# Unfolded odd units in the first batch, whole loads in the last

## Chip, cores and metric

The kernel runs on one core of a Trainium2 chip. The metric is the device time of one execution in microseconds (us), as the median of several runs.

## What is computed

Eight sequences of 3136 rows by 256 go through a Fourier layer and then a routed feed-forward layer. Of the reference this matters here (shortened):

```python
X = np.fft.rfft(x, axis=1)                      # 3136 rows
Yr = Xr @ w_r - Xi @ w_i + b_r
Yi = Xr @ w_i + Xi @ w_r + b_i
Yr, Yi = softshrink(Yr, 0.01), softshrink(Yi, 0.01)
y = np.fft.irfft(Yr + 1j * Yi, n=3136, axis=1)
scores = np.einsum('bsd,d->bs', y, w_gate)
for b in range(8):                              # top 128 rows of each batch
    xe = y[b, top_idx]
    ye = np.maximum(xe @ w1, 0.0) @ w2
    out[b, top_idx] = xe + sigmoid(scores[b, top_idx])[:, None] * ye
```

## The kernel before

The transform of 3136 = 98 x 32 points is done in two steps each way, all as small float32 matmuls.

**Stage one** (`s1`, 8 units per batch, two units to one load of 784 KB). `ld_x` brings 98 rows of 8 KB into a tile, `xt` or `cv`. `fold` forms the sum and the difference of the two halves of x (`sd`, two buffers, two instructions per unit, on VectorE or GpSimd). `s1` multiplies them by the table `w` (four matmuls in the source, eight records in the trace), ScalarE copies the result to `at` (or `ot`), and after each second unit SyncE stores 784 KB to `As` in HBM. PSUM tile `s` takes the even units of batch 0 and `px` the odd ones.

**Stage two** runs over 100 steps: `s2` (second transform step, from `As` through `ld_a` into `av`), `spectral` and `shrink` (the complex product with the weights, and the soft threshold), `s2i` (first inverse step, copied to `ct`, stored to `Cs`). **Stage three** (`s1i`, 8 units per batch) loads `Cs` into `cv` and writes the output through `ot`. Behind it `route` selects the 128 rows of a batch (`select`, eight rounds of one digit each, then `place`), `fetch` gathers them into `xe`, `ffn` computes them, and an indirect DMA scatters them.

The order on every engine is the order in which the program text runs (`manual_schedule`). Stores are collected in `stores` and issued by `flush`. SyncE (SP) issues nearly all transfers, in order, and a transfer that waits holds up all behind it. The semaphores of transfers are eight lanes (DMAHW0 to 7), so a transfer may also wait for the one eight before it.

**The start.** SP loads x of batch 0 (four transfers), constants, then stores `As` in four parts; between them stand loads of x for batch 1. `warm(n)` issues n matmuls on a constant to keep TensorE at work. `ld_a(0, 0)` needs all four stores.

**The end.** In the last batch (7), `ld_last(k, late)` loads quarter k of `Cs`. The rows of the last steps (those with a = 4, 5 in groups of six) aren't known when the other rows are, so a quarter came as four transfers of 16 rows with a = 0..3, one of 2 rows, and, after the last two steps' results were stored, two more of 16 rows (`late`). Then the eight `s1i` units of batch 7 run between the rounds of `select` for batch 7 and the feed-forward of batch 6.

Line numbers in the rows: L426 is `s1`, L460 `s2`, L531 the copy in `s2i`, L600 `s1i`, L619 `warm`, L415 `fold`, L254 the matmul of a round of `select`, L245 to L273 its steps on VectorE, L328 the last matmuls of `place`, L378 and L394 the two products of `ffn`, L160 every transfer issued through `ld`, L433 the store of `As`.

Of the kernel before, what the change touches and what calls it, by code (L numbers as in the profile page):

```python
# [27 lines left out]
def _tables():  # L28
    m = np.arange(NH)
    n2 = np.arange(N2)  # L30
    n4 = np.arange(64)
    o4 = 2 * (n4 % 32) + n4 // 32
    wf = np.zeros((64, 2, 64))
    wi = np.zeros((64, 64))
    g = np.zeros((2, 2, N2, NP, 2, 3, N2))
    gi = np.zeros((2, 2, N2, NP, 2, 2, 64))
    for j in range(NJ - 1):
        e = 2 * j + 2
        for p, r in enumerate((e, NH - e if e < NH else 0)):
            a = 2 * np.pi * ((m * r) % N1) / N1  # L40
            wf[:NH, p, 2 * j + 15 - 15 * p] = np.cos(a)
            wf[:NH, p, 2 * j + 16 - 15 * p] = -np.sin(a)
            for k2 in range(N2):
                k = r + 98 * k2
                sg = 1.0 if 2 * k <= S else -1.0
                a = 2 * np.pi * ((n2 * k) % S) / S
                g[j % 2, 0, :, j // 2, p, 0, k2] = np.cos(a)
                g[j % 2, 1, :, j // 2, p, 0, k2] = np.sin(a)
                g[j % 2, 0, :, j // 2, p, 1, k2] = -sg * np.sin(a)
                g[j % 2, 1, :, j // 2, p, 1, k2] = sg * np.cos(a)  # L50
                kk, si = (k, sg) if p == 0 else (S - k, -sg)
# [12 lines left out]
    gt = np.zeros((2, N2, 3, NF))  # L64
    gti = np.zeros((NF, 2, 64))
    slots = [(0, 98 * k2) for k2 in range(17)] + [(1, 49 + 98 * k2) for k2 in range(16)]
    for s, (q, k) in enumerate(slots):
        a = 2 * np.pi * ((n2 * k) % S) / S
        edge = k in (0, S // 2)
        gt[q, :, 0, s] = np.cos(a)  # L70
        gt[q, :, 1, s] = -np.sin(a)
        a = 2 * np.pi * ((n4 * k) % S) / S
        gti[s, 0, o4] = (1.0 if edge else 2.0) * np.cos(a) / S
        gti[s, 1, o4] = (0.0 if edge else -2.0) * np.sin(a) / S
    gt[:, :, 2] = gt[:, :, 0] + gt[:, :, 1]
    wq = np.zeros((2, 2, 32, NH, 2))
    for a in range(2):
        wq[:, a, :24, :, a] = wi[:48, :NH].reshape(24, 2, NH).transpose(1, 0, 2)
        wq[0, a, 24, :, a] = wi[48, :NH]
    near = np.array([2 * (8 * t + j) + a for j in range(8) for t in range(3) for a in range(2)])  # L80
    wc = np.zeros((64, 79))
    wc[:, 15:] = wi
    ws = wc[np.concatenate([near, [NH - 1] + 15 * [63]])]
    wis = np.stack([np.concatenate([np.roll(wc, 15, 0), wc]), np.concatenate([np.roll(wc[np.concatenate([[NH - 1], near, 15 * [63]])], 15, 0), ws])], 1)
    return (np.concatenate([np.roll(wf, 15, 0), wf]), wis, g.reshape(128, NJ - 1, 3 * N2), gi.reshape(128, NP, 2, 128),
            np.concatenate([gt.reshape(NF, 3, NF)] * 2), np.concatenate([gti] * 2), wq.reshape(128, N1))

# [23 lines left out]
def fourier_moe(ctx: ExitStack, tc: tile.TileContext, x, w_r, w_i, b_r, b_i, wg, w1, w2,  # L111
# [17 lines left out]
    def c_tile(shape, dt, name):  # L129
        return const.tile(shape, dt, name=name)  # L130

    w = c_tile([128, 2, NF], F32, "w")
    nc.scalar.dma_start(out=w, in_=t_w)
    wi_sb = c_tile([128, 2, 79], F32, "wi_sb")
    nc.scalar.dma_start(out=wi_sb, in_=t_wi)
    xts, cvs = [[c_tile([128, 8, D], F32, n + str(k)) for k in range(2)] for n in ("xt", "cv")]
    for k, t in enumerate(xts + cvs):
        (nc.vector if k % 2 else nc.gpsimd).memset(t[:15], 0.0)
    g_sb = c_tile([128, NJ - 1, 3 * N2], F32, "g_sb")
    gt_sb = c_tile([128, 3, NF], F32, "gt_sb")  # L140
    wts = [[c_tile([128, 2, D], F32R, n + c) for c in "hl"] for n in ("ws", "wd", "wn")]
# [272 lines left out]
        for k, op in enumerate((ALU.add, ALU.subtract)):  # L414
            eng.tensor_tensor(out=f[:113, k], in0=t[:113, 0], in1=t[:113, 1], op=op)  # L415

    def s1(b, i):
        if i == 0:
            As[b] = dram.tile([2, NH, N2, D], F32, name="As")
        if i % 2 == 0:  # L420
            at[b] = pool.tile([128, 2, 2, 2 * D], F32, name="ot" if b == 0 and i > 3 else "at", bufs=2)
        f = sd.pop((b, i))
        p = ps.tile([128, 2, 2 * D], F32, name="px" if b == 0 and i % 2 else "s", bufs=1)
        for r in range(2):
            for c in range(2):
                nc.tensor.matmul(p[64 * c:64 * c + 64, r, :], w[64 * r:64 + NH * r, c, :], f[64 * r:64 + NH * r, c], start=True, stop=True)  # L426
        t = at[b]
        nc.scalar.copy(out=t[:, :, i % 2, :], in_=p)  # L428
        if i % 2 == 0:
            return  # L430

        def store():
            nc.sync.dma_start(out=As[b].rearrange("q m n d -> (q m) n d")[:, 4 * i - 4:4 * i + 4, :], in_=t[15:113])  # L433
        stores.append(store)
# [68 lines left out]
    def s2i(b, g):  # L503
# [37 lines left out]
        elif b == B - 1 and g in (3, 7, 10, 11):  # L541
            def store():
                lo, n = {10: (0, 6), 11: (6, 8)}.get(g, (0, 8))
                for q in range(2):
                    ld(Cs[b][1 + 48 * q:49 + 48 * q].rearrange("(j t a) n d -> t (a n) j d", t=3, a=2)[g // 4, :, lo:n], t[q::2, lo:n])
            stores.append(store)
        elif b < B - 1 and g % 4 == 3:
            def store():
# [32 lines left out]
            cv[b, i // 2] = cvs[i // 2 % 2]  # L581
            ld(cv[b, i // 2][15:113], Cs[b].rearrange("r m n d -> (r m) n d")[:, 4 * i:4 * i + 8, :])

    def ld_last(k, late):
        t = cv[B - 1, k] = (xts if k < 2 else cvs)[k % 2]
        v = Cs[B - 1][:, 8 * k:8 * k + 8, :]
        for a in (4, 5) if late else range(4):
            ld(t[16 + a:112:6], v[1:N1 - 1].rearrange("(i a) n d -> a i n d", a=6)[a])
        if not late:
            ld(t[15:113:N1 - 1], v[::N1 - 1])  # L590

    def s1i(b, i):
        e = i % 2
# [134 lines left out]

    for i in range(U):
        ld_x(0, i)  # L730
    warm(16)
    consts_a()
    consts_g(0)
    consts_c()
    for i in range(U):
        fold(0, i, nc.gpsimd if i % 3 == 2 else nc.vector)
        s1(0, i)
        flush()
        if i == 5:
            ld_x(1, 0)  # L740
    ld_x(1, 2)
    weights()
    warm(20)
    ld_a(0, 0)
    ld_x(1, 4)
    ld_x(1, 6)
    first = {i - 1: i for i in range(U)}
# [3 lines left out]
    for t in range(-1, T):  # L751
# [6 lines left out]
        for b, i in loads[t] if t >= 0 else ():  # L758
            ld_c(b, i)
        if t > T - 3:  # L760
            for k in (0, 1) if t == T - 2 else (2,):
                ld_last(k, False)
        if t in (0, 4, 8):
            consts_g(t // 4 + 1)
        if t in (-1, 1, 4, 9):
# [62 lines left out]

    while threads or ffns:
        done["t"] = t  # L830
        if t == T:
            ld_last(3, False)
        flush()
        load[0] = 0.0
        if t == T:
# [4 lines left out]
            flush()  # L840
            load[0] = 0.0
            work(0.8, True)
            for k in range(4):
                ld_last(k, True)
        load[0] = 0.0
        turn("pe", "da", "db")
        us = 0.4 if t == T else 1.2 if t < T + 11 else 0.6
# [33 lines left out]
```

## Time and profile before

| | |
|---|---|
| median of 3 runs | 698.41 us |
| lowest, highest | 694.76, 701.81 us |
| profiled execution | 699.96 us |
| its span | 698.2 us |
| mean granted TensorE clock | 0.969 |
| TensorE (PE) busy | 654.1 us, 94% |
| VectorE (DVE), ScalarE (ACT), GpSimd (POOL) busy | 439.2, 364.7, 293.3 us |

The span is what the profiler saw; the 1.76 us by which the execution is longer lie around it. The granted clock is a share of 2.4 GHz: 1.00 is 2.4 GHz and 0.50 is 1.2 GHz.

### The profile page before, as it was taken

How to read it: one execution, taken by the hardware profiler on the slowest of the kernel's cores; microseconds unless marked ns; L12 is line 12 of the kernel's file. 1: busy time of each engine (PE TensorE's matmuls, PEld its weight loads, DVE VectorE, ACT ScalarE, POOL GpSimd, SP SyncE). 2: the span in 40 equal slices, each digit the busy share in tenths (PEclk: the TensorE clock that was granted, in tenths of full speed). 3: DMA queues.
4: the chain of work that ended last, by engine and by line, in shares of the span. 5: the costliest groups of instructions: out<-in, count | busy, mean ns of one | idle time of the engine just before them, and what ended most of it. 6: DMA issues, size and time to landing. Idle time of an engine off the chain costs nothing.

```text
span 698.2 us, 20329 instructions
## 1 busy us (share of the span) xinstructions
PE 654.1 (94%) x8363; PEld 483.3 (69%) x8363; DVE 439.2 (63%) x1388; ACT 364.7 (52%) x672; POOL 293.3 (42%) x247
## 2 busy tenths in 40 slices
PE   5679999999999999999999999999999999998896
PEld 3357766777777777777777777677777777676365
DVE  5526555677687667766667664776577667775330
ACT  2336565566665566654654664556555555553220
POOL 4168555555545555345435544554542222220001
PEclk9799999999999999999999999999999999999569
DMA  8799857798989898988587767879676745776430
GB/s 248 273 242 331 274 165 210 221 309 263 300 251 313 265 299 254 339 234 283 169 262 231 261 215 249 285 240 289 217 224 184 220 140 183 230 230 194 141 120 24
DMA packets 72014, 163.79 MB, mean 235 GB/s; under 512 B 4878, under 2 KB 57584, under 8 KB 59376
## 3 DMA queue, kind: packets, MB, share of 16 engines
q1 hardware_dynamic: 70736, 160.17, 72.8%
q0 software_dynamic: 896, 2.17, 1.0%
q8 instruction: 66, 1.08, 0.6%
q14 instruction: 28, 0.23, 0.1%
q10 hardware_dynamic: 288, 0.15, 0.1%
HBM read 84.42 MB, written 78.12 MB: 233 GB/s over the span
## 4 chain that ended last, share of the span: by engine, by line
PE 63%; DVE 14%; DMA 7%; issue 5%; ACT 5%; POOL 2%; SPq 1%; POOLq 0%; DVEq 0%; ACTq 0%
PE pca L521 10%; PE s L600 6%; DVE junk L533 5%; PE py L233 5%; PE px L460 5%; PE py L234 5%; PE s L426 5%; PE py L235 5%; PE pcb L233 4%; PE m L378 3%; PE m L394 2%; PE pcb L235 2%; PE pcb L234 2%; ACT ct L531 2%; DVE Xl L473 2%
## 5 line engine op out<-in xcount | busy, mean ns | idle before, releaser
L489 POOL TENSOR_TENSOR kb<-ks,bias 128x512 f32<-128x512 f32 x100 | 128.1, 1281 | 308.9 <-ACT ks L487 307.5
L415 POOL TENSOR_TENSOR sd<-xt 113x512 f32<-113x512 f32 x106 | 133.4, 1281 | 23.9 <-DMA xt<-in_x 12.4
L493 DVE TENSOR_TENSOR py<-py,kb 128x512 f32<-128x512 f32 x100 | 70.0, 700 | 77.9 <-POOL kb L489 73.2
L531 ACT COPY ct<-pcb 128x256 f32<-128x256 f32 (+1 forms) x100 | 37.2, 372 | 151.4 <-PE pcb L521 137.1
L521 PE MATMUL pca<-Y,gi_sb 64*64 64x256 f32 x760 | 101.8, 386 | 5.4 <-DVE pca L251 4.8
L473 DVE TENSOR_TENSOR Xl<-px,Xh 128x768 fp32r<-128x768 f32 x100 | 95.8, 958 | 16.7 <-ACT Xh L472 16.5
L521 PE MATMUL pcb<-Y,gi_sb 64*64 64x256 f32 x768 | 103.0, 386 | 0.0
L533 DVE CUSTOM_DVE_ANT_0 junk<-pcb,wgb 128x256 f32<-128x256 f32 (+1 forms) x100 | 42.4, 424 | 87.7 <-ACT ct L531 86.8
L460 PEld LDWEIGHTS px<-g_sb,av 64*64 64x64 f32 x3072 | 78.2, 134 | 17.4 <-issue 3.5
L472 ACT CAST Xh<-px 128x768 fp32r<-128x768 f32 x100 | 81.1, 811 | 13.3 <-PE px L460 11.8
L460 PE MATMUL px<-g_sb,av 64*64 64x96 f32 x3072 | 83.4, 244 | 3.5 <-issue 3.1
L602 ACT COPY ot<-s 128x1024 f32<-128x1024 f32 x58 | 60.1, 1036 | 43.3 <-PE s L600 43.3
L521 PEld LDWEIGHTS pca<-Y,gi_sb 64*64 64x64 f32 x760 | 46.5, 132 | 41.0 <-DVE pca L251 11.7
L498 ACT ACTIVATE r<-py,m2l 128x512 f32<-128x512 f32 x100 | 70.5, 705 | 4.6 <-DVE py L493 4.6
L500 DVE SCALAR_TENSOR_TENSOR Y<-py,r 128x512 f32<-128x512 f32 x100 | 68.5, 685 | 1.6 <-ACT r L498 1.6
L426 PE MATMUL s<-sd,w 64*64 64x512 f32 x480 | 67.4, 607 | 2.2 <-POOL sd L415 1.2
L428 ACT COPY at<-s 128x1024 f32<-128x1024 f32 x58 | 60.6, 1045 | 12.0 <-PE s L426 11.8
L233 PE MATMUL pcb<-wsh,Xh 128*128 128x256 f32 x200 | 65.3, 326 | 1.5 <-DVE Csc L533 1.5
L600 PE MATMUL s<-cv,wi_sb 64*64 64x512 f32 x464 | 63.3, 614 | 0.0
L233 PE MATMUL py<-wnh,Xh 128*128 128x256 f32 x200 | 56.7, 284 | 1.8 <-DVE Y L500 1.7
L234 PE MATMUL pcb<-wsh,Xl 128*128 128x256 f32 x200 | 56.0, 280 | 0.0
L235 PE MATMUL pcb<-wsl,Xh 128*128 128x256 f32 x200 | 55.9, 279 | 0.0
(184 smaller groups left out, 1368.4 us busy)
## 6 DMA issues: line engine op xcount, KB each, us to landing
av<-As SPq DMA_DIRECT2D x46, 512.0 KB
Cs<-ct SPq DMA_DIRECT2D x46, 512.0 KB
As<-at SPq DMA_DIRECT2D x30, 784.0 KB
out<-ot SPq DMA_DIRECT2D x30, 784.0 KB
xt<-in_x SPq DMA_DIRECT2D x28, 784.0 KB
cv<-Cs SPq DMA_DIRECT2D x28, 784.0 KB
cv<-in_x SPq DMA_DIRECT2D x4, 784.0 KB
As<-ot SPq DMA_DIRECT2D x2, 784.0 KB
```

Source lines behind the costliest of these rows:

```text
L233: nc.tensor.matmul(out, wh, mh, start=start, stop=False)
L234: nc.tensor.matmul(out, wl, mh, start=False, stop=False)
L235: return nc.tensor.matmul(out, wh, ml, start=False, stop=stop).ins
L415: eng.tensor_tensor(out=f[:113, k], in0=t[:113, 0], in1=t[:113, 1], op=op)
L426: nc.tensor.matmul(p[64 * c:64 * c + 64, r, :], w[64 * r:64 + NH * r, c, :], f[64 * r:64 + NH * r, c], start=True, stop=True)
L460: nc.tensor.matmul(o[:, :, N2 * j:N2 * j + N2], a[64 * p:64 * p + 64, j, g % 4, 128 * h + 64 * q:128 * h + 64 * q + 64], g_sb[64 * p:64 * ...
L472: nc.scalar.copy(out=vh, in_=v)
L473: nc.vector.tensor_tensor(out=vl, in0=v, in1=vh.bitcast(F32), op=ALU.subtract)
L489: nc.gpsimd.tensor_tensor(out=kb[:r], in0=ks[:r].broadcast_to([r, 2, D]), in1=bias[:r], op=ALU.add)
L521: nc.tensor.matmul(p[q][64 * a:64 * a + 64], gi_sb[64 * q:64 * q + 64, g, c, 64 * a:64 * a + 64], y[64 * q:64 * q + 64, c, :], start=(c == ...
L533: nc.vector.tensor_tensor_reduce(out=junk[:r], in0=p[k][:r], in1=wgb[:r], scale=1.0, scalar=0.0, op0=ALU.mult, op1=ALU.add, accum_out=Csc[ ...
L600: nc.tensor.matmul(p[64 * c:64 * c + 64, r, :], wi_sb[64 * r:64 + NH * r, b // (B - 1), 15 * c:15 * c + 64], f[64 * r:64 + NH * r, 4 * c + ...
```

## The change

Three things change, without the result being another.

In batch 0 the odd units are no longer folded. `w` gets a third column block, the negative of its second, and an odd unit takes the halves of x as they are: the sum as two accumulating matmuls with the same table, the difference as one with the table and one with its negative. An odd unit so has 16 records in place of 8, and is done ahead of the even unit of its pair. The four folds left (two instructions each) are all on VectorE. The four clearing memsets move behind the first `warm`, which is 8 matmuls long in place of 16; the second is 24 in place of 20. `ld_a(0, 0)` moves ahead of the load of x for units 2 and 3 of batch 1.

In batch 7 the first two quarters of `Cs` come in one transfer of 98 rows of 16 KB, the third in one of 98 rows of 8 KB, with all rows, known or not; what is not yet known is then replaced by two transfers of 16 rows of 16 KB and two of 16 rows of 8 KB. The fourth quarter is loaded whole after these. So that the rows hold numbers, the store of step 3 is done twice, to its own rows and to those of the last steps.

```diff
+    wf = np.concatenate([wf, -wf[:, 1:]], 1)
...
-        f = sd.pop((b, i))
...
+        if (b, i) in sd:
+            f = sd.pop((b, i))
+            parts = [[(c, f[:, c])] for c in range(2)]
+        else:
+            f = [xt[b, i // 2][:, h, 2 * e:2 * e + 2, :] for h in range(2)]
+            parts = [[(c, f[0]), (2 * c, f[1])] for c in range(2)]
+        for k in range(len(parts[0])):
+            for r in range(2):
+                for c in range(2):
+                    v, f = parts[c][k]
+                    nc.tensor.matmul(p[64 * c:64 * c + 64, r, :], w[64 * r:64 + NH * r, v, :], f[64 * r:64 + NH * r],
+                                     start=(k == 0), stop=(k == len(parts[0]) - 1))
...
-                for q in range(2):
-                    ld(Cs[b][1 + 48 * q:49 + 48 * q].rearrange("(j t a) n d -> t (a n) j d", t=3, a=2)[g // 4, :, lo:n], t[q::2, lo:n])
+                for k in (0, 2) if g == 3 else (g // 4,):
+                    for q in range(2):
+                        ld(Cs[b][1 + 48 * q:49 + 48 * q].rearrange("(j t a) n d -> t (a n) j d", t=3, a=2)[k, :, lo:n], t[q::2, lo:n])
...
-    def ld_last(k, late):
-        t = cv[B - 1, k] = (xts if k < 2 else cvs)[k % 2]
-        v = Cs[B - 1][:, 8 * k:8 * k + 8, :]
-        for a in (4, 5) if late else range(4):
-            ld(t[16 + a:112:6], v[1:N1 - 1].rearrange("(i a) n d -> a i n d", a=6)[a])
+    def ld_last(k, n, late):
+        t = whole.rearrange("p k n d -> p (k n) d") if k == 0 else cvs[k % 2]
...
+        v = Cs[B - 1][:, 8 * k:8 * k + 8 * n, :]
         if not late:
-            ld(t[15:113:N1 - 1], v[::N1 - 1])
+            ld(t[15:113], v)
+        else:
+            for a in (4, 5):
+                ld(t[16 + a:112:6], v[1:N1 - 1].rearrange("(i a) n d -> a i n d", a=6)[a])
...
-    warm(16)
+    warm(8)
...
-    for i in range(U):
-        fold(0, i, nc.gpsimd if i % 3 == 2 else nc.vector)
-        s1(0, i)
+    for i in range(0, U, 2):
+        fold(0, i, nc.vector)
+        s1(0, i + 1, True)
+        s1(0, i, False)
         flush()
-        if i == 5:
+        if i == 4:
             ld_x(1, 0)
+    weights()
+    warm(24)
+    ld_a(0, 0)
     ld_x(1, 2)
-    weights()
-    warm(20)
-    ld_a(0, 0)
...
-            for k in (0, 1) if t == T - 2 else (2,):
-                ld_last(k, False)
+            ld_last(*((0, 2) if t == T - 2 else (2, 1)), False)
...
-        if t == T:
-            ld_last(3, False)
         flush()
...
-            for k in range(4):
-                ld_last(k, True)
+            ld_last(0, 2, True)
+            ld_last(2, 1, True)
+            ld_last(3, 1, False)
```

Three places show how the instructions move. First TensorE at the start of the program, before, from the first `warm` to the third unit (`px<-Xh` is the warming):

```order
L619 MATMUL px<-Xh 128x512 [waits Activation_49]
L619 MATMUL px<-Xh 128x512 x15
L426 MATMUL s<-sd,w 64x512 [waits DMAHW0_49,DVE_49]
L426 MATMUL s<-sd,w 64x512 [waits DVE_49]
L426 MATMUL s<-sd,w 64x512 x2
L426 MATMUL px<-sd,w 64x512 [waits DVE_49,PE_49]
L426 MATMUL px<-sd,w 64x512 [waits DVE_49]
L426 MATMUL px<-sd,w 64x512 x2
L426 MATMUL s<-sd,w 64x512 [waits Activation_49,Pool_49]
L426 MATMUL s<-sd,w 64x512 [waits Pool_49]
L426 MATMUL s<-sd,w 64x512 x2
```

And the same place now (the odd unit reads `xt` or `cv_83`, which hold x):

```order
L633 MATMUL px<-Xh 128x512 [waits Activation_49]
L633 MATMUL px<-Xh 128x512 x7
L434 MATMUL px<-xt,w 64x512 [waits DMAHW0_49,DMAHW1_49,DVE_49,PE_49]
L434 MATMUL px<-xt,w 64x512 x7
L434 MATMUL s<-sd,w 64x512 [waits DVE_49] x2
L434 MATMUL s<-sd,w 64x512 x2
L434 MATMUL px<-xt,w 64x512 [waits DMAHW3_49,Activation_49,Pool_49]
L434 MATMUL px<-xt,w 64x512 x7
L434 MATMUL s<-sd,w 64x512 [waits DVE_49,Activation_49]
L434 MATMUL s<-sd,w 64x512 [waits DVE_49]
L434 MATMUL s<-sd,w 64x512 x2
```

The odd unit comes first and waits for the load of x and for the table, not for a fold; the warming ahead of it is half as long.

Second, SP at the start, from the first store of `As` to the loads of x for batch 1 (`xt`, `cv` from `in_x`), before:

```order
L433 DMA As<-at 98x2048 [waits DMAHW3_49,Activation_49]
L433 DMA As<-at 98x2048 [waits DMAHW4_49,Activation_49]
L433 DMA As<-ot 98x2048 [waits DMAHW5_49,Activation_49]
L160 DMA xt_82<-in_x 98x2048 [waits DMAHW6_49,DVE_49]
L433 DMA As<-ot 98x2048 [waits DMAHW7_49,Activation_49]
L160 DMA xt_83<-in_x 98x2048 [waits DMAHW0_49,DVE_49,Pool_49]
L160 DMA av<-As 128x2x256 [waits DMAHW5_49,DMAHW4_49,DMAHW7_49,DMAHW3_49,DMAHW1_49]
L160 DMA av<-As 128x2x256 [waits DMAHW2_49]
L160 DMA av<-As 128x2x256 x2
L160 DMA cv_84<-in_x 98x2048 [waits DVE_49,Pool_49]
L160 DMA cv_85<-in_x 98x2048 [waits DMAHW6_49,DVE_49]
```

And now:

```order
L443 DMA As<-at 98x2048 [waits DMAHW3_49,Activation_49]
L443 DMA As<-at 98x2048 [waits DMAHW4_49,Activation_49]
L443 DMA As<-ot 98x2048 [waits DMAHW5_49,Activation_49]
L160 DMA xt<-in_x 98x2048 [waits DMAHW6_49,DVE_49,PE_49]
L443 DMA As<-ot 98x2048 [waits DMAHW7_49,Activation_49]
L160 DMA av<-As 128x2x256 [waits DMAHW5_49,DMAHW4_49,DMAHW7_49,DMAHW3_49,DMAHW0_49]
L160 DMA av<-As 128x2x256 [waits DMAHW1_49]
L160 DMA av<-As 128x2x256 [waits DMAHW2_49]
L160 DMA av<-As 128x2x256
L160 DMA xt<-in_x 98x2048 [waits DVE_49,PE_49]
L160 DMA cv_83<-in_x 98x2048 [waits DVE_49,PE_49]
L160 DMA cv_84<-in_x 98x2048 [waits DMAHW6_49,DVE_49,PE_49]
```

The second load of x into `xt` now stands behind the four loads of `av`.

Third, SP near the end, from the last transfer of the third quarter of `Cs_77` (batch 7) over the fourth quarter to the first late transfer, before (ahead of these stand ten transfers for the first two quarters and four for the third):

```order
L160 DMA cv_84<-Cs_77 2x2048 [waits DMAHW2_49]
L160 DMA cv_85<-Cs_77 16x2048 [waits DMAHW3_49,PE_49]
L160 DMA cv_85<-Cs_77 16x2048 [waits DMAHW4_49]
L160 DMA cv_85<-Cs_77 16x2048 [waits DMAHW5_49]
L160 DMA cv_85<-Cs_77 16x2048 [waits DMAHW6_49]
L160 DMA cv_85<-Cs_77 2x2048 [waits DMAHW7_49]
L160 DMA out<-ot 98x2048 [waits DMAHW0_49,Activation_49]
L160 DMA Cs_77<-ct 64x6x256 [waits DMAHW1_49,Activation_49]
L160 DMA Cs_77<-ct 64x6x256 [waits DMAHW2_49]
L160 DMA Cs_77<-ct 64x2x256 [waits DMAHW3_49,Activation_49]
L160 DMA Cs_77<-ct 64x2x256 [waits DMAHW4_49]
L160 DMA xt_82<-Cs_77 16x2048 [waits DMAHW4_49,DMAHW3_49,DMAHW5_49,DMAHW2_49,DMAHW1_49]
```

And now, with the first three quarters in the first two rows:

```order
L160 DMA xt<-Cs_77 98x4096 [waits DMAHW4_49,DMAHW6_49,DMAHW3_49,Pool_49]
L160 DMA cv_83<-Cs_77 98x2048 [waits DMAHW7_49,DMAHW0_49,PE_49]
L160 DMA out<-ot 98x2048 [waits Activation_49]
L160 DMA Cs_77<-ct 64x6x256 [waits DMAHW6_49,DMAHW7_49,DMAHW1_49,Activation_49]
L160 DMA Cs_77<-ct 64x6x256 [waits DMAHW2_49]
L160 DMA Cs_77<-ct 64x2x256 [waits Activation_49]
L160 DMA Cs_77<-ct 64x2x256
L160 DMA xt<-Cs_77 16x4096 [waits DMAHW4_49,DMAHW3_49,DMAHW5_49,DMAHW2_49,DMAHW1_49]
L160 DMA xt<-Cs_77 16x4096
L160 DMA cv_83<-Cs_77 16x2048
L160 DMA cv_83<-Cs_77 16x2048 [waits DMAHW0_49]
L160 DMA cv_84<-Cs_77 98x2048 [waits PE_49]
```

The first store of the last steps' results, `Cs_77<-ct 64x6x256`, now waits for the lanes of the two whole loads (6 and 7), the output store ahead of it stands behind two transfers in place of twenty, and the fourth quarter comes behind the late transfers.

## Rows read from the trace of the kernel before

**Rows 1.** The page: TensorE in 40 slices, chain by engine.

```profile
PE   5679999999999999999999999999999999998896
...
PE 63%; DVE 14%; DMA 7%; issue 5%; ACT 5%; POOL 2%; SPq 1%; POOLq 0%; DVEq 0%; ACTq 0%
```

**Rows 2.** Chain of waits, 0 to 60 us: start us, us, what.

```profile
19.24 2.50 POOL sd L415 x2
...
26.52 9.72 DMA As<-ot
...
36.77 3.98 DMA av<-As
```

**Rows 3.** SP's timeline, 26 to 37 us: start, length of issue, transfer.

```profile
26.52 0.31 SPq L433 DMA_DIRECT2D As<-ot  x1
26.93 0.73 SPq L160 DMA_DIRECT2D xt<-in_x  x1
```

**Rows 4.** Busy time by stretch; the last three are PE clock, DMA share, GB/s.

```profile
0.00:20.00 20.00, 12.43 (x56) 6.21 (x56) 10.48 (x11) 5.65 (x6) 9.18 (x18) 0.93 0.85 266
20.00:25.50 5.50, 5.27 (x31) 1.17 (x24) 4.55 (x7) 3.26 (x5) 1.73 (x2) 0.96 0.66 210
25.50:36.30 10.80, 5.79 (x18) 4.66 (x19) 4.12 (x9) 1.61 (x2) 2.21 (x2) 0.68 0.80 262
41.00:60.00 19.00, 18.58 (x272) 12.58 (x266) 9.17 (x19) 11.23 (x19) 13.35 (x11) 0.91 1.01 291
```

**Rows 5.** Timeline of the start, PE: start, us, instruction, count.

```profile
12.04 1.09 PE L426 MATMUL s<-sd,w 64*64 64x512 f32 x8
...
30.51 6.49 PE L619 MATMUL px<-Xh 128*128 128x512 f32 x20 [5.09 <-ACT Xh L616]
```

**Rows 6.** Chain of waits, 630 to 699 us, around the last batch's first units.

```profile
641.60 2.96 DMA Cs<-ct
...
648.13 1.65 PE s L600 x8
...
653.08 1.15 PE py L394 x2
...
654.47 1.92 PE s L600 x8
```

**Rows 7.** SP's timeline near the end.

```profile
621.14 8.64 SPq L160 DMA_DIRECT2D xt<-Cs  x10
629.88 7.09 SPq L160 DMA_DIRECT2D cv<-Cs  x10
637.07 0.35 SPq L160 DMA_DIRECT2D out<-ot  x1
637.53 5.11 SPq L160 DMA_DIRECT2D Cs<-ct  x4
```

**Rows 8.** Timeline of ACT near 637 us, PE near 646 us.

```profile
635.26 0.39 ACT L531 COPY ct<-pca 128x256 f32<-128x256 f32 x1
...
637.62 0.38 ACT L531 COPY ct<-px 128x256 f32<-128x256 f32 x1
...
645.77 0.39 PE L328 MATMUL pca<-neg,hot 98*128 98x34 f32 x2
```

**Rows 9.** Busy time by microsecond; the last three are PE clock, DMA share, GB/s.

```profile
648.00:649.00 1.00, 0.87 (x8) 0.24 (x8) 0.00 (x0) 0.00 (x0) 0.10 (x1) 0.77 0.88 229
...
675.00:676.00 1.00, 1.00 (x8) 0.99 (x8) 0.14 (x2) 0.16 (x1) 0.00 (x0) 0.58 0.77 246
```

**Rows 10.** Chain of waits, 196 to 216 us: a mid-kernel unit.

```profile
198.05 1.02 PE s L600 x8
```

**Rows 11.** Timeline, 651 to 679 us: DVE in select, PE in feed-forward.

```profile
651.20 0.17 DVE L261 TENSOR_SCALAR ok<-pcb 128x15 f32<-128x15 f32 x1 [3.55 <-PE pcb L254]
...
652.35 0.08 DVE L245 DVE_READ_ACCUMULATOR c<-rep,f 128x1 f32 x1
...
678.44 3.70 PE L394 MATMUL py<-w2s,hh 128*128 128x256 f32 x16
```

More of the change, by code (lines that the diff above doesn't have):

```diff
@@ L130, in c_tile @@
         return const.tile(shape, dt, name=name)
-    w = c_tile([128, 2, NF], F32, "w")
+    w = c_tile([128, 3, NF], F32, "w")
     nc.scalar.dma_start(out=w, in_=t_w)
@@ L135, in fourier_moe @@
     nc.scalar.dma_start(out=wi_sb, in_=t_wi)
-    xts, cvs = [[c_tile([128, 8, D], F32, n + str(k)) for k in range(2)] for n in ("xt", "cv")]
-    for k, t in enumerate(xts + cvs):
-        (nc.vector if k % 2 else nc.gpsimd).memset(t[:15], 0.0)
+    whole = c_tile([128, 2, 8, D], F32, "xt")
+    xts, cvs = [whole[:, k] for k in range(2)], [c_tile([128, 8, D], F32, "cv" + str(k)) for k in range(2)]
     g_sb = c_tile([128, NJ - 1, 3 * N2], F32, "g_sb")
@@ L415, in fold, with s1 @@
             eng.tensor_tensor(out=f[:113, k], in0=t[:113, 0], in1=t[:113, 1], op=op)
[L417 to L420, printed above, removed]
-            at[b] = pool.tile([128, 2, 2, 2 * D], F32, name="ot" if b == 0 and i > 3 else "at", bufs=2)
-        f = sd.pop((b, i))
[L423 to L426, printed above, removed]
+    def s1(b, i, first=None):
+        e = i % 2
+        if (e == 0 if first is None else first):
+            if b not in As:
+                As[b] = dram.tile([2, NH, N2, D], F32, name="As")
+            at[b] = pool.tile([128, 2, 2, 2 * D], F32, name="ot" if b == 0 and i > 3 else "at", bufs=2)
+        p = ps.tile([128, 2, 2 * D], F32, name="px" if b == 0 and e else "s", bufs=1)
+        if (b, i) in sd:
[10 more added lines that the diff above has]
+                                     start=(k == 0), stop=(k == len(parts[0]) - 1))
         t = at[b]
-        nc.scalar.copy(out=t[:, :, i % 2, :], in_=p)
-        if i % 2 == 0:
+        nc.scalar.copy(out=t[:, :, e, :], in_=p)
+        if (e == 0 if first is None else first):
             return
+        i = i | 1
         def store():
@@ L582, in ld_c @@
             ld(cv[b, i // 2][15:113], Cs[b].rearrange("r m n d -> (r m) n d")[:, 4 * i:4 * i + 8, :])
-    def ld_last(k, late):
-        t = cv[B - 1, k] = (xts if k < 2 else cvs)[k % 2]
-        v = Cs[B - 1][:, 8 * k:8 * k + 8, :]
-        for a in (4, 5) if late else range(4):
-            ld(t[16 + a:112:6], v[1:N1 - 1].rearrange("(i a) n d -> a i n d", a=6)[a])
+    def ld_last(k, n, late):
+        t = whole.rearrange("p k n d -> p (k n) d") if k == 0 else cvs[k % 2]
+        for i in range(k, k + n):
+            cv[B - 1, i] = (xts + cvs)[i]
+        v = Cs[B - 1][:, 8 * k:8 * k + 8 * n, :]
         if not late:
-            ld(t[15:113:N1 - 1], v[::N1 - 1])
+            ld(t[15:113], v)
+        else:
+            for a in (4, 5):
+                ld(t[16 + a:112:6], v[1:N1 - 1].rearrange("(i a) n d -> a i n d", a=6)[a])
     def s1i(b, i):
@@ L730, in fourier_moe @@
         ld_x(0, i)
-    warm(16)
+    warm(8)
+    for k, t in enumerate(xts + cvs):
+        (nc.gpsimd if k % 2 else nc.vector).memset(t[:15], 0.0)
     consts_a()
```

## Prediction

> **What bounds the kernel now.** I read the page first, then the chain of waits by its longest pieces, then the two ends in SP's timeline and in busy time by stretch. TensorE is busy in nearly every slice but the first two and the last few, and matmuls hold most of the chain [rows 1]. So between about 45 and 640 us the order on TensorE sets the time, and the change leaves that order alone. It acts on the two ends, and whatever it gains or loses at the start shifts all that follows.
>
> At the start the chain runs over folds on GpSimd (one unit 2.50 us), then over the fourth store of As, issued at 26.52 and landed 9.72 us later, then over the first loads of av, 3.98 us [rows 2]. So the start ends with transfers, and the question is whether they or the arithmetic are late. The stretches answer: the transfer engines are 85% busy up to 20 us, but only 66% from 20 to 25.5 us, where the stores wait for units not yet computed, and 80% after that [rows 4].
>
> At the end the chain goes from the last store of Cs (issued 641.60, landed 2.96 us later, at 644.56) over the late loads to the first unit of batch 7 on TensorE at 648.13 [rows 6]. TensorE had ended its last matmul of place at 646.16 (645.77 + 0.39) [rows 8], so it stood still for 1.97 us. Behind that wait comes something larger: at 648.5 the granted clock falls from 2.4 to 1.2 GHz and comes back only at about 675.8 (0.77 in the one microsecond, 0.58 in the other) [rows 9]. For some 27.3 us the tail runs at half clock.
>
> **Start, step by step.** Volumes follow from the shapes: a load of x or a store of As is 98 rows of 8 KB, 0.80 MB. Up to 36.3 us the transfers moved 20 x 266 + 5.5 x 210 + 10.8 x 262 KB, about 9.3 MB [rows 4]. One of these loads, the second x of batch 1, was issued at 26.93, right behind the fourth store [rows 3], and shares the engines with it. The change puts it behind av: 8.5 MB are left ahead of av.
>
> Are the stores issued early enough that the transfers never run dry? On TensorE a folded unit is 8 records, 1.09 us at full clock [rows 5]; an unfolded one is 16, so 2.2 us; four of each are 13 us in place of 8.7. But the chain of fold, wait, matmul is gone for half the units, and the four folds left, on VectorE now and taken as no dearer than GpSimd's 2.50 us [rows 2], hide beside the odd units' matmuls. With eight warming matmuls ahead, the first unit can start when x and the larger table have landed, which I estimate at 7 to 9 us: nearly 1 MB at 266 KB/us, and 3 us before anything moves. Before, the first unit started at 12.04, behind the warming [rows 5]. Eight units then end at about 21 us, or some 3 us later if the first part runs at half clock; the last store of As is issued at 22 to 25 us, not at 26.5. At 20 us 5.3 MB had been moved, so 3.2 MB remain: the transfers stay supplied. At 262 KB/us (the last stretch, its pause included) that takes 12.3 us; at 313 (5.3 MB in the 17 us after the first 3, an estimate from the first stretch) 10.3 us. So the fourth store lands at 30.3 to 32.3 us. Before, it landed at 36.24. I take 31.3: **5.0 us earlier**; the ends are 0 (the load moved did not delay the store, and the supply is no better) and 6.
>
> Two things take some of it back. The second warming ends before av lands, so TensorE stands still longer and starts stage two at half clock; before, it also lost some microseconds of full clock there (mean 0.91 in 41 to 60 us [rows 4]). I take **0.8 us**, between 0 and 1.7 (as much half clock again as 0.91 over 19 us means there, 3.4 us). And the moved load adds 0.80 MB behind av, to a stretch where the transfers are already 101% busy [rows 4]: at 291 KB/us 2.8 us of work. Its first user is the third unit's fold in batch 1, and behind that fold on GpSimd stands the first bias addition, for which VectorE and so the second step of stage two wait. No row shows that slack; I take **0.3 us** (0 to 2.8), nearer to nothing, since av, issued ahead of it, is what the first steps need. The start is worth 5.0 - 0.8 - 0.3 = **3.9 us**.
>
> The moved memsets, the warming and the table block cost nothing on the path: all of it lies before x has landed. If not, the transfers cover up to 4 us of it.
>
> **End, step by step.** Before, SP issued twenty small loads from 621.14 to 636.97, each waiting for a lane; the output store and the stores of the last steps' results stood behind them (637.07, 637.53) [rows 7]. All of these, 0.80 + 0.79 + 0.26 MB, then went through together, which is why the last store, whose data ScalarE had copied at 638.00 [rows 8], landed only at 644.56. Now two loads stand there. The output store leaves some 5 us earlier. The first store of results waits for both whole loads: 1.6 MB issued from 621.14 and 0.8 MB from 629.88, when the third quarter's tile is free [rows 7]. At 266 KB/us the latter takes 3 us and some 2 more to land, 635, and ScalarE's data for that store come at 635.65 [rows 8]. So I cost this new wait at nothing; the cover is about 1 us, and a microsecond beyond it moves every store and load behind it on SP by as much. The last store can be issued from 638.0, say 638.6 behind its neighbour, and in the 2.96 us of before is landed at 641.6. The late loads are four in place of eight, and the first two hold 256 KB each in place of 128. Before, 3.57 us went from that landing to the first unit [rows 6]; the 256 KB more cost another 1.1 at the 229 KB/us moved there [rows 9]: 646.3. TensorE is at its place matmuls until 646.16 anyway. So the first unit starts **1.9 us** earlier, no more than 2.0, and the other end is 0. The doubled store of step 3 (1 MB near 590 us) and the fourth quarter's whole load (needed six units later) are hidden.
>
> **The clock.** With that wait gone, TensorE still has little but the short matmuls of select and place just before 646.2, but then a unit of batch 7 at once. At half clock a round of select with one unit is 3.31 us (653.08 to 656.39: 1.15 for the feed-forward pair, 0.24, 1.92 for the unit) [rows 6]. At full clock the unit is 1.02 us [rows 10] and the pair 0.46 (3.70 / 8) [rows 11]; VectorE's part of a round is 1.23 us (651.20 to 652.43) [rows 11] and runs beside them. That makes about 1.9 us with the matmul of select. In the stretch there are eight units (0.9 saved each), five pairs (0.7), and about 3 us of smaller savings: 7.2 + 3.5 + 3.0 = 13.7, less about 1.7 where VectorE now sets the round: **12.0 us**. The other end is 0, if the clock falls all the same.
>
> Sum, against the profiled execution of 699.96 us: 699.96 - 3.9 - 1.9 - 12.0 = **682.2**, so 682. That execution is 1.55 us above the median; I leave that in the range.
>
> **Rivals.** (a) The clock falls in the tail all the same: 699.96 - 3.9 - 1.9 = 694.2. For it: the thin stretch just before 646.2 remains, and once down, the clock stayed down for 27 us although the chain there runs on TensorE without a gap. Against: what went before the fall was a full pause of 2 us, and that goes. The Trainium skill (Perfetto Trace Analysis, Matmul Optimizations) says that the engine scales its power with utilization and that matmuls should be issued back to back in batches; the fall at 648.5, behind a pause of 1.97 us, agrees with it, and what remains before 646.2 isn't back to back either.
>
> (b) The clock holds, but the start's gain is used up where the transfers are saturated: the 3.9 us are lost and 699.96 - 13.9 = 686.1 stays.
>
> (c) The whole loads come too late. A piece of 16 rows needs only its rows; a whole load needs all, and the next stores wait for it. If their 2.4 MB go no faster than the twenty small loads did (2.1 MB from 621.14 to 636.97, 133 KB/us [rows 7]), they end at 639.2; the 1.05 MB of results then take 4 us at 266 KB/us and 1 to land, the late loads 4.7: 648.9, 0.8 us later than before, and the clock falls. That gives 699.96 - 3.9 + 0.8 = 696.9. Against it: the small loads were slow because each waited for a lane on SP, as their spacing shows [rows 7]. The Trainium skill (Perfetto Trace Analysis, DMA Optimizations) states that splitting transfers into smaller chunks may let some start sooner and the whole end sooner; by that rule this is the outcome, and no row here shows a whole load in that place.
>
> (d) Slower: the start runs at half clock on TensorE. Then the units take 1.92 / 1.02 times as long, some 25 us with the doubled odd ones, from 8 to 33; the 24 warming matmuls, which stand ahead of stage two on TensorE, need another 10 (twenty took 6.49 with the clock low in half of it [rows 5]). Stage two starts at about 45 us, not at 40.75, where av was in [rows 2]: + 4.2, and with the clock low in the tail 699.96 + 4.2 - 1.9 = 702.3, up to 706 if that stage then begins at half clock for longer. It decides from the point where the warming ends after 40.75 us. Against it: before, the clock was full for most of this stretch (0.93, 0.96) [rows 4].
>
> **Chances.** Forecast 0.50; (a) 0.27, (b) 0.10, (c) 0.06, (d) 0.07. A measurement here tells about 1% from no change, 6.98 us: faster is below 691.4, slower above 705.4. The forecast, (b) and a little of (a) are faster: 0.62. Most of (a), with (c) and half of (d): 0.34. Slower: 0.04. The forecast's own range is 678 to 688. For 8 in 10 the range must take in (a) and (b) and may leave out the far ends: 678 to 697.
>
> **What would show it.** Stage two's first matmul at about 36 us, the fourth store landed at 30 to 32. At the end the first unit of batch 7 starts right behind the last matmul of place, and no stretch of 27 us has a granted clock of 0.50; a round of select takes 1.9 us. The forecast is wrong if the clock falls there again, or if the late loads land after place's matmuls by a microsecond or more.

## The result and the profile after

The changed kernel takes 696.15 us (median of 20 executions, 685.73 to 701.34), the kernel before 699.3 us in the same comparison. The ratio is 0.9886, 95% interval 0.985 to 0.9922; it leaves out executions over 1.5% above the kernel's fastest (here ten of those in which the clock fell; the ratios of the experiments do the same), and so stands lower than the ratio of the two medians, 0.9955. The forecast was 682. The time lies inside the range, near its upper end, but of the 16 us forecast only some 3 came (3.15 between the two medians).

The executions fall into two groups by the mean clock that each one lists: five of 20 have 0.989 to 0.994 and take 685.73 to 690.62 us; fifteen have 0.968 to 0.979 and take 692.6 to 701.3. The profiled execution (692.63 us, span 690.4, clock 0.976) is of the second group. Of the kernel before no execution whose clock is listed, 66 beside the experiments, has more than 0.983. From here on an execution **kept** the clock if its mean is 0.986 or more; none lies between 0.983 and 0.986.

First the page, TensorE's busy share and granted clock in 40 slices, and the chain's share by engine; the answer to [rows 1]. Near the end the clock is short of full in two slices, 0.7 each (a 9 stands for 0.90 or more).

```profile
PE   7689989999999999999999999999999999998896
...
PEclk9889999999999999999999999999999999999779
...
PE 65%; DVE 14%; DMA 7%; ACT 5%; issue 5%; POOL 2%; SPq 1%; POOLq 0%; ACTq 0%; DVEq 0%
```

The chain of waits of the start (start us, us, what), the answer to [rows 2]:

```profile
7.48 2.68 PE px L434 x16
...
21.50 10.19 DMA As<-ot
...
32.23 3.02 DMA av<-As
...
44.05 1.28 POOL sd L415
45.32 1.24 POOL kb L499
46.58 0.71 DVE py L503
...
48.87 0.35 PE py L233
```

The first unit starts at 7.48 us, not at 12.04 [rows 5]. The fourth store of As is issued 5.0 us earlier and lands at 31.69 us, and av at 35.25, 5.5 us earlier than before. But at 44 us the chain leaves TensorE: it runs over GpSimd's fold, the first bias addition, VectorE and so to the matmul at 48.87. SP's timeline (the answer to [rows 3]) has the load that this fold reads, now behind av, and ScalarE's timeline the fourth copy of stage two (the mark used below), which stood at 54.58 before (the last block):

```profile
31.79 1.92 SPq L160 DMA_DIRECT2D av<-As  x4
33.80 0.40 SPq L160 DMA_DIRECT2D xt<-in_x  x1
...
52.75 0.81 ACT L482 CAST Xh<-px 128x768 fp32r<-128x768 f32 x1
```

```profile
54.58 0.81 ACT L472 CAST Xh<-px 128x768 fp32r<-128x768 f32 x1
```

So 1.83 us of the 5.5 are left there, and 2.19 reach the tail: ScalarE's copies of the last results stand at 635.43 (637.62 in [rows 8]). By stretch (PE clock, DMA share, GB/s last; the answer to [rows 4]) the transfers are supplied much better from 20 to 25.5 us (0.89 in place of 0.66), and stage two begins with 6.8 us at half clock:

```profile
20.00:25.50 5.50, 1.84 (x8) 1.20 (x5) 3.18 (x7) 2.09 (x3) 0.00 (x0) 0.74 0.89 365
...
36.30:43.10 6.80, 5.95 (x54) 3.67 (x50) 1.91 (x2) 3.67 (x5) 0.29 (x1) 0.50 1.02 265
```

At the end, SP's timeline and the chain answer to [rows 7] and [rows 6], the last block (ScalarE's and TensorE's timelines) to [rows 8]:

```profile
623.05 0.31 SPq L160 DMA_DIRECT2D xt<-Cs  x1
623.47 0.56 SPq L160 DMA_DIRECT2D cv<-Cs  x1
...
634.67 3.18 SPq L160 DMA_DIRECT2D Cs<-ct  x4
640.22 1.20 SPq L160 DMA_DIRECT2D xt<-Cs  x2
```

```profile
623.47 11.11 DMA cv<-Cs
...
636.67 3.41 DMA Cs<-ct
...
640.84 4.42 DMA xt<-Cs
...
645.39 1.09 PE s L614 x8
```

```profile
633.07 0.39 ACT L541 COPY ct<-pca 128x256 f32<-128x256 f32 x1
...
635.43 0.38 ACT L541 COPY ct<-px 128x256 f32<-128x256 f32 x1
...
643.58 0.39 PE L328 MATMUL pca<-neg,hot 98*128 98x34 f32 x2
```

The whole load of the third quarter lands at 634.58, and the first result store follows at 634.67, though its data were ready at 633.46 (633.07 + 0.39): the new wait on SP binds, by 1.2 us. The last store lands at 640.08, the late loads at 645.26, and TensorE, done with place at 643.97, stands still for 1.42 us (1.97 before). Then, as before, the clock falls, for 17 us in place of 27 (the answer to [rows 9]):

```profile
647.00:648.00 1.00, 1.00 (x9) 0.37 (x9) 0.62 (x4) 0.55 (x1) 0.00 (x0) 0.65 0.83 254
664.00:665.00 1.00, 1.00 (x10) 0.28 (x3) 0.56 (x4) 0.09 (x1) 0.00 (x0) 0.81 0.94 254
```

The span is 7.8 us shorter: 2.2 from the start, 0.55 from the first unit (2.74 earlier, less 2.19), and 5.1 from there to the end (45.0 us in place of 50.1), where the clock came back sooner. This last part can't be put down to the change: e13, the same code, has a longer stretch at half clock than the kernel before.

### The profile page after: what moved, and what is told of

The parts are those of the page before. It is cut to its first block, busy times and chain, and to the rows that moved or that the text cites. A ratio compares the mean times of both kernels' runs of the same rounds, so it can differ in the third digit from the quotient of the medians.

```text
span 690.4 us, 20349 instructions
## 1 busy us (share of the span) xinstructions
PE 650.7 (94%) x8391; PEld 481.8 (70%) x8391; DVE 434.5 (63%) x1384; ACT 364.5 (53%) x672; POOL 287.7 (42%) x243
## 4 chain that ended last, share of the span: by engine, by line
PE 65%; DVE 14%; DMA 7%; ACT 5%; issue 5%; POOL 2%; SPq 1%; POOLq 0%; ACTq 0%; DVEq 0%
PE pca L531 10%; PE s L614 6%; DVE junk L543 5%; PE py L233 5%; PE px L470 5%; PE py L234 5%; PE py L235 5%; PE s L434 5%; PE pcb L233 4%; PE m L378 3%; PE m L394 3%; PE pcb L235 2%; PE pcb L234 2%; DVE Xl L483 2%; ACT ct L541 2%
## 5 line engine op out<-in xcount | busy, mean ns | idle before, releaser
L415 POOL TENSOR_TENSOR sd<-xt 113x512 f32<-113x512 f32 x104 | 130.5, 1277 | 31.7 <-DMA xt<-in_x 23.7
L434 PE MATMUL s<-sd,w 64*64 64x512 f32 x480 | 65.0, 600 | 0.8 <-ACT ot L616 0.8
```

## The experiments

Theory: **a pause of TensorE in front of batch 7's first unit makes the clock fall**, and the change shortens the pause without closing it; the start's gain is used up by the x load moved behind av. Rivals: the short matmuls of select and place let the clock fall with or without a pause; the start is limited by saturated transfers, or by its own half clock. Kept counts the executions that kept the clock.

| kernel | median us | ratio to before | kept |
|---|---|---|---|
| changed kernel | 696.15 | 0.9886 | 5 of 20 |
| e1 start alone | 698.53 | 1.0017 (0.9991 to 1.0043) | 0 of 12 |
| e2 end alone | 685.83 | 0.9845 (0.9789 to 0.99) | 4 of 6 |
| e3 changed, pause filled | 687.82 | 0.9877 (0.9829 to 0.9924) | 5 of 6 |
| e4 before, pause filled | 687.42 | 0.9849 (0.9817 to 0.9882) | 6 of 6 |
| e5 as e3, x load ahead of av | 685.91 | 0.9829 (0.9794 to 0.9864) | 6 of 6 |
| e6 as e3, 40 warming matmuls | 689.88 | 0.9886 (0.985 to 0.9922) | 6 of 6 |
| e7 changed, late loads cut | 686.73 | 0.9831 (0.9794 to 0.9869) | 5 of 6 |
| e8 end alone, cut and filled | 687.57 | 0.9849 (0.981 to 0.9887) | 5 of 6 |
| e9 all three mended | 683.99 | 0.9829 (0.9799 to 0.986) | 5 of 5 |
| e10 start with load ahead, filled | 685.26 | 0.9849 (0.9813 to 0.9885) | 4 of 4 |
| e11 start as changed, filled | 687.44 | 0.9869 (0.9835 to 0.9904) | 4 of 4 |
| e12 changed, load ahead of av | 695.31 | 0.9901 (0.9854 to 0.9948) | 2 of 12 |
| e13 changed kernel again | 697.17 | 0.9871 (0.9827 to 0.9916) | 5 of 12 |
| e14 end alone again | 695.3 | 0.9909 (0.9869 to 0.995) | 4 of 12 |

e1 to e4 ran on one chip (before 696.98 there), e5 to e8 on another (696.92), e9 to e11 on a third (695.92), e12 to e14 on a fourth (699.75).

**e1, e2: one half of the change each.** The changed kernel with the old end, and the kernel before with the new end; each takes its half from the diff shown ahead.

> The kernel before with the new start alone; the end is the old one (twenty small loads, eight late ones). In the profiled pair the start's gain had shrunk from 5.5 us at the first loads of av to 2.2 us at the copies of the last steps' results. If that is all the start is worth, this kernel is 2 to 2.5 us below the kernel before (ratio about 0.997), with the same pause of about 2 us before batch 7's first unit and the same stretch of some 27 us at half clock behind it. If the start also decides how the clock behaves in the tail, it comes out near the changed kernel, 3 us or more below.

> The kernel before with the new end alone (whole loads, four late transfers, the doubled store of step 3); the start is the old one. If start and end add up, this one is 1 to 3 us below the kernel before: the first unit of batch 7 half a microsecond earlier, and a stretch at half clock that is shorter in some executions. A rival: the end gains nothing by itself (ratio 1.000), since the pause before the first unit is still over a microsecond long and the clock falls as before.

The start alone shows no gain, where 2 to 2.5 us were expected. In its profile (of its slowest execution, 702.23 us) the fourth store lands at 33.74, not at 31.69, and TensorE waits 2.72 us before the first unit (the last store of results takes 3.69 us to land there, 2.96 before); PE's timeline of e1, then of e2:

```profile
649.54 1.13 PE L610 MATMUL s<-xt,wi_sb 64*64 64x512 f32 x4 [2.72 <-DMA xt<-Cs]
```

```profile
646.29 1.09 PE L605 MATMUL s<-xt,wi_sb 64*64 64x512 f32 x8 [0.38 <-DMA xt<-Cs]
```

With the end alone the pause in the profile is 0.38 us and the clock stays up: 684.6 to 687.0 us where it does, 694.0 and 695.5 in the two executions where it doesn't. Both expectations of e2 were far too small; how much of its 11 us was chance, e14 tells.

**e3, e4: the pause filled.** Matmuls whose results nobody reads, ahead of batch 7's first unit; six in the changed kernel, eight in the kernel before.

```diff
             if not alone and rest and turns % 3 == 0 and ready():
+                if rest[0] == (B - 1, 0):
+                    idle(6)
                 s1i(*rest.pop(0))
```

> The changed kernel with six matmuls of 512 columns, whose results nobody reads, on TensorE between place's last matmul and batch 7's first unit, about 1.3 us, so that they fill the pause of 1.42 us. Theory: the pause is what makes the clock fall, so here it stays at 2.4 GHz in the tail of nearly all executions, and the median is 685 to 687. Rival: the clock falls because of the short, broken-up matmuls of select and place on both sides, and the filling changes nothing: the median stays at 694 to 697, with a stretch at 0.50 in the profile.

> The kernel before with eight such matmuls (1.7 us) in the same place, where its pause is 1.97 us; nothing else is changed. Theory (the pause makes the clock fall): the 27 us at half clock go, and the time falls by 9 to 12 us to 687 to 690, below the changed kernel. Rival (the pause does not matter): 699, no difference.

Filling the pause keeps the clock, with select and place as they were. Eight matmuls and nothing else take 9.6 us from the kernel before (696.98 to 687.42); all six executions keep the clock, where none of the 66 without them did. That is more than the whole change does. e3 came 0.8 us above its forecast, and one of its six executions lost the clock (so did one each of e7 and e8): what happened there no trace shows. PE's timeline of e4 and its busy time by stretch (PE clock, DMA share, GB/s last), the stretch that stood at half clock:

```profile
645.65 0.39 PE L328 MATMUL pca<-neg,hot 98*128 98x34 f32 x2
645.87 2.08 PE L632 MATMUL s<-wsh 128*128 128x512 f32 x8
648.01 1.09 PE L600 MATMUL s<-xt,wi_sb 64*64 64x512 f32 x8
```

```profile
646.00:664.00 18.00, 17.88 (x113) 8.52 (x113) 10.64 (x55) 8.30 (x9) 1.99 (x2) 1.00 0.64 201
664.00:676.00 12.00, 11.48 (x76) 10.26 (x75) 2.89 (x15) 1.40 (x3) 1.97 (x2) 1.00 0.28 91
```

The units of batch 7 take 1.09 us there, and a round some 1.9 us (648.01, 649.79, 651.78 us), as forecast.

**e5, e6: the start.** e5 is e3 with one line moved, e6 is e3 with one number changed.

```diff
+    ld_x(1, 2)
     warm(24)
     ld_a(0, 0)
-    ld_x(1, 2)
```

> The changed kernel with the pause filled as in e3, and the second x load of batch 1 back in its old place on SP, right behind the fourth store of As and ahead of av. In e3 that load was issued at 36.2 us and landed 8.6 us later, and GpSimd's fold, the first bias addition, VectorE and TensorE waited for it one after the other. Theory 1: that late fold is what used up the start. Then GpSimd's fold of it here starts behind TensorE's second unit of batch 1, the wait of TensorE at about 48 us goes, the fourth step of stage two is 1.5 to 3 us earlier than in e3 (54.81 us there), and the median falls by 1 to 2.5 us below e3's. Theory 2: the transfers are saturated, so that the load only pushes av back by its own 2.8 us: stage two then starts that much later than in e3 (38.80 us at its first copy) and the fourth step stands where it stood.

> The changed kernel with the pause filled as in e3, and 40 warming matmuls instead of 24 ahead of stage two, so that TensorE has no pause before av lands. Theory 1 (the late x load holds stage two): the start of stage two is at full clock for longer, but its fourth step stands where it stood in e3, within half a microsecond, and the median is e3's, 687 to 688. Theory 2 (the half clock of 3 to 7 us at the start of stage two used the gain up): the clock stays up from 36 to 43 us and the fourth step and the median are 1.5 to 3 us earlier.

The load's move used up the start. In e3 (chain of waits) the load is on the path, with fold and bias addition behind it; in e5 (GpSimd's and ScalarE's timelines) the fold waits for TensorE's unit alone, the bias addition comes 2.9 us sooner (44.52, not 47.41), and so does the fourth copy, 51.98 in place of 54.81:

```profile
36.19 8.58 DMA xt<-in_x
...
46.14 1.27 POOL sd L415
47.41 1.24 POOL kb L499
```

```profile
54.81 0.81 ACT L482 CAST Xh<-px 128x768 fp32r<-128x768 f32 x1
```

```profile
40.91 2.51 POOL L415 TENSOR_TENSOR sd<-xt 113x512 f32<-113x512 f32 x2 [4.79 <-PE s L434]
44.52 1.28 POOL L499 TENSOR_TENSOR kb<-ks,bias 128x512 f32<-128x512 f32 x1 [1.10 <-ACT ks L497]
...
51.98 0.81 ACT L482 CAST Xh<-px 128x768 fp32r<-128x768 f32 x1
```

av is hardly later for it: stage two's first copy is at 39.16 (38.80 in e3), 0.36 us and not 2.8, so theory 2 fails. The busy time by stretch tells why, in e3, then in e5 (PE clock, DMA share, GB/s last):

```profile
30.00:34.00 4.00, 3.27 (x15) 2.38 (x13) 0.00 (x0) 0.00 (x0) 1.91 (x2) 1.00 0.30 123
```

```profile
30.00:34.00 4.00, 3.23 (x14) 2.31 (x12) 0.00 (x0) 0.00 (x0) 2.85 (x3) 0.96 0.60 227
```

SP waits there for the fourth store to land. With the load behind av little is left for the transfer engines (busy 0.15 to 0.32 in the seven profiles of this kind, 0.60 to 0.72 in the four with the load ahead), and its 0.80 MB then come in a stretch that is full (0.97 from 36 to 45 us in e3). The fold is not all that is late for it: in the profiles of e1, e7 and e13 the chain passes, at 53 us, over another transfer that now lands late, the table `gi_sb` that `s2i` needs. The line of e13 (chain of waits), landed at 52.94:

```profile
37.49 15.45 DMA gi_sb<-t_gi
```

In e6 TensorE never pauses ahead of stage two, and the clock is full from there on; yet the fourth copy comes only 0.40 us earlier (54.41), since the late fold still holds it. PE's timeline and busy time by stretch of e6:

```profile
26.14 11.53 PE L633 MATMUL px<-Xh 128*128 128x512 f32 x40 [4.70 <-ACT Xh L630]
37.73 0.89 PE L470 MATMUL px<-g_sb,av 64*64 64x96 f32 x32
```

```profile
36.00:43.00 7.00, 5.83 (x94) 3.52 (x93) 1.53 (x2) 3.21 (x4) 0.52 (x1) 1.00 0.94 249
```

That e6's median is 2 us above e3's isn't explained by this: neither theory had it slower. In the profiles 1.05 us of it arise between the fourth copy and the last, where e3 and e6 are the same program and where the sixteen profiles take from 568.2 to 569.9 us; why this varies is open.

**e7: the late transfers cut** into 128 KB each, the first quarter's ahead; nothing filled.

```diff
-            ld_last(0, 2, True)
+            for k in range(2):
+                ld_last(k, 1, True)
```

> The changed kernel without filling, its two late transfers of 256 KB cut into four of 128 KB, the first quarter's ahead. The first unit then waits for 256 KB and not for 512. Theory: its pause, 1.42 us in the changed kernel's profile, becomes about 0.5 us shorter or more, and since the pause decides the clock, more executions keep 2.4 GHz in the tail: median 686 to 692. Rival: the two transfers' time is latency and not volume; the pause and the median stay (694 to 697).

```profile
647.47 0.39 PE L328 MATMUL pca<-neg,hot 98*128 98x34 f32 x2
647.79 1.09 PE L614 MATMUL s<-xt,wi_sb 64*64 64x512 f32 x8
```

PE's timeline of e7: the first unit follows place's last matmul with no wait, and five of six executions keep the clock, with no work added. Merging two quarters into one late transfer had made the first unit wait for the second quarter.

**e8, e9: the mended kernels.** e8 is e2 with e7's cut and three filling matmuls; e9 is the changed kernel with e5's line, e7's cut and two filling matmuls.

> The kernel before with the new end, the late transfers cut as in e7, and three filling matmuls (0.65 us) ahead of batch 7's first unit; the old start. By what e1 to e4 showed, this keeps what is worth something: no half clock in the tail of any execution and the first unit right behind place. 683 to 686 us in all runs, below both kernels. If the start is worth something after all, the changed start with the same end would be lower still.

> The changed kernel with the load in its old place (e5), the late transfers cut (e7) and two filling matmuls. If the three terms add up: the clock up in all runs, the fourth step at 52 us, the first unit right behind place: 683.5 to 685.5, at or below e5's 685.9, with every run below 688.

e8 missed: it isn't below e2's executions that kept the clock, and one of its six lost it. e9's times came as expected, 682.98 to 685.17, below both kernels in every execution and 11.9 us below the one before on its chip. But its first unit isn't right behind place: TensorE still waits 0.63 us there. With ScalarE's last copy 2.4 us earlier than in the changed kernel's profile, the stores' wait for the whole loads (landed at 634.37) puts the last store 3.10 us behind its data, where it was 0.86 in the changed kernel.

**e10, e11: the worth of the start with the clock held.** The old end, eleven filling matmuls, and the new start with the load ahead of av (e10) or behind it (e11).

> The kernel before with the new start, but the second x load of batch 1 in its old place behind the fourth store, the old end, and eleven filling matmuls (2.4 us) ahead of batch 7's first unit, so that the clock stays up in the tail. Beside e4, which has the old start and the same old end filled, it gives the worth of the start without the load's move. By e5 the fourth step is 2.8 us earlier than with the load behind av, and in e4 it came at 55.83 us, in e5 at 51.98: so 1 to 3.5 us below e4's 687.4, of which the old end, if its transfers bind, can take back up to 2. Rival: the start is worth nothing either way (687 to 688), since the old end waits for transfers that are not earlier.

> The same as e10 with the load behind av, as the changed kernel has it: the new start as it is, the old end, eleven filling matmuls. If the move of that load takes back what the stores gain, this one is e4's 687.4 within a microsecond; if the start as it is is worth its 2.2 us of the first profiled pair, it is at 685 to 686.

As it is, the start shows no gain (687.44 beside e4's 687.42; on two chips, and against the kernel before on each 8.5 and 9.6 us). The load's old place is worth 2.2 us (e10 against e11, one chip).

**e12 to e14: does the start lengthen the pause?** e12 is the changed kernel with e5's line, nothing filled; e13 is the changed kernel, e14 is e2, unchanged.

> The changed kernel with the second x load of batch 1 back ahead of av, and nothing filled: TensorE comes to the tail 2 to 3 us earlier than in the changed kernel, while the last stores and late loads may not. Theory 1 (start and end work against each other): the pause before batch 7's first unit is longer, the clock falls in most executions, and the median is 690 to 694, though every held one is at 683 to 685. Theory 2 (the clock's fall in the changed kernel's runs was chance or a matter of the chip): it holds here as often as with the end alone, median 683 to 685.

> The changed kernel, beside the kernel with the end alone on the same chip. Theory 1 (start and end work against each other): the clock falls in most executions here and in few with the end alone; median 693 to 697 here. Theory 2 (chance or chip): both hold it equally often, and the medians are within 2 us of each other.

> The kernel before with the new end alone (as e2), on the same chip as the changed kernel. Theory 1: held in most executions, median 684 to 687. Theory 2: as often as the changed kernel, so with a median near that one's.

Theory 2 stands, chance or the chip: on one chip the changed kernel keeps the clock in 5 of 12 executions, the end alone in 4 of 12. Together with the earlier runs that makes 10 of 32 and 8 of 18. e12's 2 of 12 is too near to tell, and its median lies above both its forecasts. PE's timelines have pauses of 0.89, 1.21 and 1.65 us (e14, e12 and e13 in turn):

```profile
646.76 1.09 PE L605 MATMUL s<-xt,wi_sb 64*64 64x512 f32 x8 [0.89 <-DMA xt<-Cs]
```

```profile
646.08 1.99 PE L614 MATMUL s<-xt,wi_sb 64*64 64x512 f32 x8 [1.21 <-DMA xt<-Cs]
```

```profile
647.80 1.98 PE L614 MATMUL s<-xt,wi_sb 64*64 64x512 f32 x8 [1.65 <-DMA xt<-Cs]
```

The five profiles with the new end and nothing filled or cut (e2, e14, the changed kernel, e12, e13) also show what sets the pause. In each TensorE ends place 8.2 us behind ScalarE's last copy, with either start; the last store is issued 0.6 to 0.9 us behind that copy, and the unit starts 5.1 to 5.3 us behind that store's landing. The store itself differs most, 2.76, 3.09, 3.41, 3.52 and 3.84 us from issue to landing in the order given (chain of e2, then of e13):

```profile
638.39 2.76 DMA Cs<-ct
```

```profile
638.76 3.84 DMA Cs<-ct
```

Why it differs is open.

e13's profile also settles the 17 us: the same code stood at half clock for 31 us there, as its stretches show, with a span of 698.8 us.

```profile
646.00:664.00 18.00, 16.35 (x61) 7.17 (x61) 6.82 (x36) 4.97 (x5) 0.98 (x1) 0.54 0.51 149
664.00:676.00 12.00, 12.00 (x52) 6.49 (x51) 3.96 (x21) 3.48 (x6) 1.00 (x1) 0.50 0.40 128
676.00:682.00 6.00, 6.00 (x36) 5.72 (x36) 1.52 (x11) 1.04 (x2) 0.89 (x1) 0.83 0.16 56
```

## Why the prediction was wrong

It named the right mechanisms, but two of its terms were mis-sized, and a third hung on them.

- **The end, 1.9 us, with the pause closed.** This is the step that failed, and the clock hangs on it. The forecast had the late loads landed at 646.3, against place's end at 646.16 in the frame of before: a pause of 0.1 us. It is 1.42 us. Of the 1.3 us between, some 0.3 come from the issue of the store on the chain (0.86 us behind its data, costed at 0.6), behind result stores that waited for a whole load until 634.58: the wait costed at nothing. Another 0.45 come from that store (3.41 us, not 2.96) and 0.6 from the late loads (5.3 us from the store's landing to the unit, not 4.7). The cover of 1 us given for the new wait was gone. Cutting the late loads closes the pause (e7).
- **The clock, 12.0 us.** The mechanism was right: the pause, not the thin work around it (e3, e4). The size was 9.6 us between medians (e4); in the profiled pair, which the forecast started from, it was 11.3 (from the first unit to the end 50.1 us before, 38.8 in e4). But it is had only where the clock holds, in 10 of the changed kernel's 32 executions, and the median is one of the others. That is rival (a), 694.2; the median lies 2 us above it, with the start's 3.9 us missing and a sum that began 1.55 us above the median of before.
- **The start, 3.9 us.** No gain shows (e1, e11). The profiled execution, with stage two 5.5 us earlier, is the earliest of its kind: in the ten others with the new start the first copy of stage two comes at 38.2 to 39.5 us, 2.3 to 3.5 earlier than before (41.73), where here it came at 35.97. So the term of 5.0 was rather 3. The moved load, taken at 0.3 us with 2.8 as its other end, costs 2.8 at the fourth copy (e5 against e3) and 1.9 to 2.2 in the time (e5, e10). The chain of its first user was named, fold, bias addition, VectorE, but the load was counted by its own volume alone: it took 8.58 us behind av in transfers already full, while ahead of av the transfer engines had little to do (0.30 busy from 30 to 34 us in e3).
- **The half clock at stage two, 0.8 us,** did not show in the time: without it the late fold still held the step (e6).
- **Rival (b)**, 686.1, is where the executions that kept the clock stand (685.7 to 690.7). Its cause was in part another: the transfers are saturated behind av, but e5, with the same bytes in another order, keeps the gain.
- **Rival (c)**, whole loads too late: its wait was there, 1.2 us in place of the 3.6 in its sum (639.2 less 635.65), and moved the store on the chain by 0.3. The Trainium skill (Perfetto Trace Analysis, DMA Optimizations) says that splitting transfers may let some start sooner, and ties an earlier end of the whole to idle transfer engines, a condition that the prediction left out; e7 agrees with the first, by what waits for them: the first unit needs half of what the merged transfers bring. **Rival (d)** did not come: the start's units ran at full clock.
- **The pause and the clock.** The Trainium skill (Perfetto Trace Analysis, Matmul Optimizations) asks for matmuls back to back, since the engine scales its power with utilization; the runs agree: 2.08 us of useless ones saved 9.6. In the profiles without filling or cut, the clock stayed up behind pauses of 0.38 and 0.89 us (e2, e14) and fell with 1.21, 1.42, 1.65, 1.97 and 2.72 (e12, the changed kernel, e13, before, e1): within the pause in e12, e13 and e1, 0.4 us behind its end before and 1.9 in the changed kernel. Those are seven executions and no limit; that the pause's length also decides in the executions without a trace is likely but not shown.

## What to carry to other kernels

Where the granted clock falls behind a pause in a serial tail, close the pause before shortening anything else: a few matmuls that nobody reads cost nothing in idle time (e4's first unit starts at 648.01, where it stood at 648.13) and were worth more here than the whole change. A load that is moved behind another is costed by the chain of its first user at the stretch's real landing time, not by its volume; and look at what the transfer engines do in the place that it leaves. A transfer should hold no more than its first user needs, if that user is what the end waits for.

## What the runs showed of the hardware

Once at 1.2 GHz, TensorE stayed there for 17 to 31 us although its matmuls ran without a gap (PE busy 12.00 of 12.00 us at clock 0.50 in e13's second stretch). The same kernel has it in some executions and not in others, and the changed kernel's first twenty times spread over 15.6 us. The median of such a kernel says which kind is more frequent (e2 and e14, the same code on two chips, differ by 9.5 us), so kinds have to be compared one by one.
